# Storing a generated factor with its multiples first and its channels innermost, so that phases are made in place and lag products read a strided moving operand

## The chip, the cores and the metric

The kernel runs on one core of a Trainium2 chip. A core has five engines with queues of their own: TensorE (PE; its weight loads are shown as PEld), VectorE (DVE), ScalarE (ACT), GpSimd (POOL) and SyncE (SP), which issues most of the DMAs. Within a queue the order is fixed; between engines, semaphores order the work. The metric is the device time of one execution in microseconds (us), of which several runs are taken and the median given. Beside them one execution is profiled: every instruction with its engine, source line, tiles, start and duration.

## The reference

Two kinds of layer alternate, twice each: a state-space convolution (S4) and a gated feed-forward net, each behind a layer norm and with a residual. The sequence has L = 2048 steps, the model D = 512 channels, a channel N = 128 states.

```
dt = exp(log_dt)[:, None];  A = A_re + 1j*A_im;  Bc, Cc likewise
P = exp((dt*A)[:, :, None] * arange(L))           # D x N x L
K = einsum("dn,dnl,dn->dl", Cc, P, dt*Bc).real    # the kernel of each channel
y = irfft(rfft(pad(u)) * rfft(pad(K)))[:L] + u*Dskip
x = x + y;   x = x + (silu(n @ w_gate) * (n @ w_up)) @ w_down
```

The change touches only how K is made. It is the same in both convolution layers and is made once.

## The kernel before

A lag l from 0 to 2047 is written as l = 64 b + a', with 32 values of b and 64 of a'. For each state and channel the power exp(dt A l) is the product of a small factor g(b), which also holds C dt B, and a large factor e(a'). K is then a product over the 128 states, which lie on the partitions: for each channel a matmul of g's 32 columns with 64 columns of e, real and imaginary part. These are the **lag products** (`lags`, L486, matmuls at L493 and L494): 64 channels a chunk, two matmuls each, four channels at a time in four column groups of the array; each fp32 matmul stands as two records in the profile. The result is the PSUM tile pk.

The 512 channels are worked in eight chunks of DC = 64. For a chunk `gen_tiles` (L352) takes the tiles re and im (128 states x 64 channels x 65 multiples; two pairs that alternate, tags W0 to W3), mu, xz, mz and tu. Then, in this order:

- `turn_units` (L362), for all channels at the start: th and th32 become the phase of one step and of 32 steps, as integer fractions of a turn. VectorE multiplies by dt (L370), ScalarE copies to integer (L371), VectorE subtracts and scales (L372, L374). Before the change it is called for channels 0 to 127, 128 to 255 and 256 to 511.
- `gen_turns` (L376): VectorE makes five phases in xz (L380) and a ladder of 16 multiples of the large phase in tu (16 multiples x 64 channels): L382, then L386 three times, each doubling the number.
- `gen_trig` (L391): ScalarE makes sine and cosine: for xz (L395 to L401 with 320 elements), then for the sixteen phases into rows 33 to 48 of re and im (L399 absolute value, L400 sine, L401 cosine; 1024 elements), reading tu transposed. `gen_upper` (L404, L407): VectorE adds the sixteenth phase to all of tu. ScalarE does L399 to L401 again, into rows 49 to 64.
- `gen_exp` (L409): ScalarE writes exponentials (the magnitudes) into rows 1 to 32 of re, one row an instruction (L419), and squares (L431). `upper` (L423): squares of them into mu (L425).
- `gen_e` (L434): VectorE multiplies magnitudes and sines into the large factor, rows 0 to 63 of re and im (L440, L443, L445, L448), partly in two halves of the channels.
- `gen_g` (L451): VectorE makes g by doubling (L455 to L483). In chunks 1 to 6 the last product goes to acc (L472), and GpSimd issues a DMA that adds it to the upper half of g (L473).

Behind the lag products ScalarE copies pk to ks (L499), SyncE spreads it through DRAM into kt (L506, L508), and `spectra` (L534) multiplies kt with Fourier constants (L523), two rounds of 32 matmuls a chunk: the first of its own chunk, the second after the next chunk's lag products. Between them lie products for the norm of the weights (L326) and a block of direct products of normalised inputs (L289).

On VectorE, ScalarE, TensorE and SyncE the order is written out by hand. Up to the first lag products it is the sequence of calls from L937 on: statistics of the first 512 rows, units of phase, chunk 0's factors, normalised inputs ne (L281) for the first direct products, chunk 1's phases in between. From then on each step enters a plan with a time (`at`, L994), and the plan is sorted by time; the times only set the order. In chunk c, beginning at t, the lag products of c are issued at t, the factors of c + 1 are finished (`factors`, L1016), and phases and exponentials of c + 2 are made (`prepare`, L1001). So chunk c + 2's phases and exponentials may be written into re and im only when the lag products of c, which read the same buffers, are done.

After the eighth chunk come the weights' splitting, the convolutions of eight blocks and the feed-forward net; this is about three quarters of the time.

Of the kernel before, what the change touches and what calls it, by code (L numbers as in the profile page):

```python
# [14 lines left out]
I32 = mybir.dt.int32  # L15
AF = mybir.ActivationFunctionType
# [6 lines left out]
P = 128  # L23
# [50 lines left out]
def kernel(ctx, tc, x, a_re, a_im, b_re, b_im, c_re, c_im, log_dt, d_skip,  # L74
# [12 lines left out]
    def tl(shape, name, tag, dt=F32):  # L87
        return sb.tile(shape, dt, name=name, tag=tag, bufs=BUFS[tag])
# [263 lines left out]
    def gen_tiles(ch):  # L352
        re = tl([P, DC, 65], "re", f"W{2 * (ch % 2)}")
        im = tl([P, DC, 65], "im", f"W{2 * (ch % 2) + 1}")
        mu = tl([P, DC, 32], "mu", "n")
        xz = tl([P, 3, 5, DC], "xz", "bd")
        mz = mz2[:, ch % 2]
        tu = tl([P, 16, DC], "tu", "z", I32)
        return re, im, mu, xz, mz, tu


    def turn_units(c0, c1):  # L362


        n = c1 - c0
        cs = slice(c0, c1)
        ft = tl([P, 2, 2, n], "ft", "sg")
        fr, fk = ft[:, 0], ft[:, 1].bitcast(I32)
        for i, scale in enumerate((1.0, 32.0)):
            V.scalar_tensor_tensor(fr[:, i], th[:, cs], scale / (2.0 * math.pi), dt[:, cs], OP.mult, OP.mult)  # L370
        A.activation(fk, fr, AF.Copy)  # L371
        V.tensor_tensor(fr, fr, fk, OP.subtract)  # L372
        for i, o in enumerate((th, th32)):
            V.tensor_scalar(o[:, cs].bitcast(I32), fr[:, i], TURN, TURN / 2 - 128.0, OP.mult, OP.min)  # L374

    def gen_turns(ch, ts):  # L376

        re, im, mu, xz, mz, tu = ts
        cs = slice(ch * DC, (ch + 1) * DC)
        V.tensor_tensor(xz[:, 1].bitcast(I32), th[:, cs].bitcast(I32).unsqueeze(1).to_broadcast([P, 5, DC]),  # L380
                        am.unsqueeze(2).to_broadcast([P, 5, DC]), OP.logical_shift_left)
        V.tensor_tensor(tu[:, 0:2], th32[:, cs].bitcast(I32).unsqueeze(1).to_broadcast([P, 2, DC]),  # L382
                        am[:, 0:2].unsqueeze(2).to_broadcast([P, 2, DC]), OP.logical_shift_left)
        yield
        for n in (2, 4, 8):
            V.tensor_tensor(tu[:, n:2 * n], tu[:, 0:n], tu[:, n - 1:n].to_broadcast([P, n, DC]), OP.add)  # L386
            yield
        G.memset(im[:, :, 32], 0.0)
        yield

    def gen_trig(ts):  # L391


        re, im, mu, xz, mz, tu = ts
        A.activation(xz[:, 2], xz[:, 1].bitcast(I32), AF.Sin, scale=-TWO_PI / TURN)  # L395
        tv = tu.rearrange("p m d -> p d m")
        for c, s, turns in ((xz[:, 0], xz[:, 1], xz[:, 1].bitcast(I32)), (re[:, :, 33:49], im[:, :, 33:49], tv),
                            (re[:, :, 49:65], im[:, :, 49:65], tv)):
            A.activation(c, turns, AF.Abs)  # L399
            A.activation(s, turns, AF.Sin, scale=TWO_PI / TURN)  # L400
            A.activation(c, c, AF.Sin, scale=-TWO_PI / TURN, bias=hpi)  # L401
            yield

    def gen_upper(ts):  # L404

        tu = ts[5]
        V.tensor_tensor(tu, tu, tu[:, 15:16].to_broadcast([P, 16, DC]), OP.add)  # L407

    def gen_exp(ch, ts):  # L409


        re, im, mu, xz, mz, tu = ts
# [4 lines left out]
        G.memset(re[:, :, 0], 1.0)  # L417
        for a in sorted(LOW):
            A.activation(re[:, :, a], r_, AF.Exp, scale=32.0 * a)  # L419
            yield  # L420
        yield from squares(ts)

    def upper(ts):  # L423

        A.activation(ts[2][:, :, 1:], ts[0][:, :, 1:32], AF.Square)  # L425

    def squares(ts):

        re = ts[0]
        for st in (2, 4):  # L430
            A.activation(re[:, :, st:33:2 * st], re[:, :, st // 2:17:st], AF.Square)  # L431
            yield

    def gen_e(ts):  # L434


        re, im, mu = ts[:3]
        half = [[t.rearrange("p (g h d) a -> p g h d a", g=4, h=2)[:, :, o] for t in ts[:3]] for o in range(2)]
        for r, m, u in half:
            V.tensor_tensor(m[..., :32], m[..., 64:32:-1], r[..., :32], OP.mult)  # L440
            yield
        for r, m, u in half:
            V.tensor_tensor(r[..., :32], r[..., 64:32:-1], r[..., :32], OP.mult)  # L443
            yield
        V.scalar_tensor_tensor(im[:, :, 33:64], im[:, :, 31:0:-1], -1.0, mu[:, :, 1:], OP.mult, OP.mult)  # L445
        yield
        for r, m, u in half:
            V.tensor_tensor(r[..., 33:64], r[..., 31:0:-1], u[..., 1:], OP.mult)  # L448
            yield

    def gen_g(ch, ts, g):  # L451

        re, im, mu, xz, mz, tu = ts
# [5 lines left out]
        V.tensor_tensor(g[:, :, 0], w_, re[:, :, 64].unsqueeze(1).to_broadcast([P, 2, DC]), OP.mult)  # L459
        V.tensor_tensor(tmp[:, :, 0], w_[:, ::-1], im[:, :, 64].unsqueeze(1).to_broadcast([P, 2, DC]), OP.mult)  # L460
# [25 lines left out]
    def lags(ts, g):  # L486
        re, im = ts[:2]
        pk = pbig([P, 16, 64], "pk")
        for d in range(DC):
            grp, dd = d % 4, d // 4  # L490
            d = 16 * grp + dd
            o = pk[32 * grp:32 * grp + 32, dd, :]
            PE.matmul(o, lhsT=g[:, 0, :, d], rhs=re[:, d, 0:64], start=True, stop=False, tile_position=(0, 32 * grp))  # L493
            PE.matmul(o, lhsT=g[:, 1, :, d], rhs=im[:, d, 0:64], start=False, stop=True, tile_position=(0, 32 * grp))  # L494
        return pk
# [440 lines left out]
    with tc.manual_schedule(engines={mybir.EngineType.Activation, mybir.EngineType.DVE, mybir.EngineType.PE}):  # L936
# [29 lines left out]
        take(fw[1], 1)  # L966
        stats_x = stats(x1, 4, 1.0)
        take(fw[2], 1)
        for g in (gg, ge, gg, ge, gg, ge, gg, ge, gg, tn, gg, tn, gg, tn, gg, tn, gg, tn):
            take(g, 1)  # L970
        tr = gen_trig(ts[1])
        take(tr, 2)
        gen_upper(ts[1])
# [7 lines left out]
        take(tr, 1)  # L981
        take(fw[5], 1)
        for g in (gg, ge, ge, gg, ge, ge):
            take(g, 1)
# [16 lines left out]
        def prepare(c, t):  # L1001
# [7 lines left out]
            for k in range(5):  # L1009
                at(t + 14.4 + 0.4 * k, steps["turns"])  # L1010
            for k in range(3):
                at(t + 17.4 + 2.2 * k, tr)
            at(t + 21.5, lambda: gen_upper(ts[c]))
            at(t + 12.6, steps["exp"], 100)

        def factors(c, t):  # L1016
# [7 lines left out]
            for k in range(4):  # L1024
                at(t + 0.2 + 2 * k, gg, 2)
                if k < 2:
                    at(t + 0.3 + 2 * k, ge, 1)
# [220 lines left out]
```

## Time and profile before

| | us |
|---|---|
| median of 3 runs (lowest, highest) | 1217.76 (1215.12, 1218.78) |
| the profiled execution's own time | 1216.14 |
| its span, first to last instruction | 1214.3 |
| busy: PE / DVE / ACT / POOL | 1097.5 / 1007.3 / 623.5 / 92.8 |
| mean granted TensorE clock | 0.975 |

A row of waits names the engine, tile and line that waited, what released it, then the total in us, the times and the longest. A row of a timeline gives the start, the duration (of several instructions where xN stands at the end), engine, line, operation, output and inputs with shapes, and in brackets how long the engine had been idle and what ended that. A group row gives the count, total busy us and mean ns of one. A stage row gives start:end, length, and each engine's busy us with the number of instructions, then granted clock, DMA share and GB/s. Durations of neighbouring instructions overlap somewhat, so that a pair takes less than the sum of both.

### The profile page before, as it was taken

How to read it: one execution, taken by the hardware profiler on the slowest of the kernel's cores; microseconds unless marked ns; L12 is line 12 of the kernel's file. 1: busy time of each engine (PE TensorE's matmuls, PEld its weight loads, DVE VectorE, ACT ScalarE, POOL GpSimd, SP SyncE). 2: the span in 40 equal slices, each digit the busy share in tenths (PEclk: the TensorE clock that was granted, in tenths of full speed). 3: DMA queues.
4: the chain of work that ended last, by engine and by line, in shares of the span. 5: the costliest groups of instructions: out<-in, count | busy, mean ns of one | idle time of the engine just before them, and what ended most of it. 6: DMA issues, size and time to landing. Idle time of an engine off the chain costs nothing.

```text
span 1214.3 us, 24571 instructions
## 1 busy us (share of the span) xinstructions
PE 1097.5 (90%) x10008; PEld 866.0 (71%) x10008; DVE 1007.3 (83%) x1612; ACT 623.5 (51%) x1205; POOL 92.8 (8%) x151
## 2 busy tenths in 40 slices
PE   0677888889989997999999999989999999999998
PEld 0555676767778684868687777858686776867875
DVE  3878888889879989899899999998997699984221
ACT  6398888993455255355745353564531553325111
POOL 1001111111000001001100000020100010000000
PEclk9988889889989999999999999999999999999999
DMA  5145665665748334732334444433435154312000
GB/s 207 44 149 129 144 142 151 152 174 165 256 140 260 118 117 144 183 116 92 86 113 141 124 157 129 133 102 116 124 120 152 60 133 132 117 57 45 14 23 18
DMA packets 136531, 151.17 MB, mean 124 GB/s; under 512 B 75473, under 2 KB 83665, under 8 KB 136418
## 3 DMA queue, kind: packets, MB, share of 16 engines
q1 hardware_dynamic: 129314, 126.47, 34.8%
q0 software_dynamic: 7104, 23.14, 7.3%
q8 instruction: 78, 1.28, 0.4%
q14 instruction: 35, 0.29, 0.1%
HBM read 101.85 MB, written 31.46 MB: 110 GB/s over the span
## 4 chain that ended last, share of the span: by engine, by line
PE 35%; DVE 27%; issue 4%; DMA 4%; ACT 2%; SPq 1%; POOL 0%; DVEq 0%; ACTq 0%; POOLq 0%
PE pgu L894 6%; PE pgu L895 6%; PE pgu L897 6%; DVE t L762 5%; DVE yk L765 4%; PE py L909 4%; PE py L910 4%; PE py L911 3%; PE pi L781 3%; PE pf L273 3%; DVE yk L762 2%; DMA mix<-nn 2%; DVE z L229 2%; DVE sg L901 2%; DVE bb L229 1%
## 5 line engine op out<-in xcount | busy, mean ns | idle before, releaser
L894 PE MATMUL pgu<-mix,wsl 128*128 128x256 f16 x1280 | 299.7, 273 | 5.3 <-DVE sg L901 2.7
L895 PE MATMUL pgu<-mix,wsl 128*128 128x256 f16 x1280 | 299.7, 273 | 0.0
L897 PE MATMUL pgu<-mix,wsl 128*128 128x256 f16 x1280 | 195.7, 273 | 0.0
L909 PE MATMUL py<-wsl,hh 128*128 128x512 f16 (+1 forms) x352 | 134.3, 381 | 8.8 <-DVE xg L914 7.1
L895 PEld LDWEIGHTS <-wsl 128*128 128x128 f16 x1280 | 125.5, 98 | 22.7 <-issue 6.5
L894 PEld LDWEIGHTS <-wsl 128*128 128x128 f16 x1280 | 125.3, 98 | 16.2
L897 PEld LDWEIGHTS <-wsl 128*128 128x128 f16 x1280 | 125.3, 98 | 15.0
L911 PE MATMUL py<-wsl,hl 128*128 128x512 f16 (+1 forms) x352 | 134.3, 382 | 0.3 <-DVE hl L903 0.3
L910 PE MATMUL py<-wsl,hh 128*128 128x512 f16 x320 | 122.0, 381 | 0.0
L762 DVE TENSOR_TENSOR t<-uu,w 128x1024 f32<-128x1024 f32 x96 | 117.7, 1226 | 2.7 <-DMA w<-wdr 2.5
L765 DVE TENSOR_TENSOR yk<-yk,t 128x1024 f32<-128x1024 f32 x96 | 117.7, 1226 | 0.3
L900 ACT ACTIVATE sg<-pgu,sc 128x512 f32<-128x512 f32 x80 | 54.6, 683 | 119.7 <-PE pgu L897 115.1
L901 DVE SCALAR_TENSOR_TENSOR sg<-pgu,sc,sg 128x512 f32<-128x512 f32 x80 | 60.3, 753 | 55.5 <-ACT sg L900 55.3
L523 PE MATMUL pw<-kt,ek 128*128 128x256 f32 (+1 forms) x384 | 93.6, 381 | 0.0
L902 ACT ACTIVATE hh<-sg 128x512 f16<-128x512 f32 x80 | 50.1, 626 | 77.2 <-DVE sg L901 77.1
L781 PE MATMUL pi<-yl,mix 128*128 128x256 f16 x576 | 78.9, 273 | 5.0 <-DVE yl L229 2.7
L493 PE MATMUL pk<-re,g 128*32 128x64 f32 x1024 | 46.2, 275 | 38.0 <-DVE re L448 33.1
L523 PEld LDWEIGHTS pw<-kt,ek 128*128 128x128 f32 x384 | 70.8, 194 | 8.3
L273 PE MATMUL pf<-z,eh 128*128 128x256 f16 x576 | 74.9, 273 | 0.0
L762 DVE TENSOR_TENSOR yk<-u,w0r 128x1024 f32<-128x1024 f32 x56 | 68.7, 1226 | 1.5 <-ACT u L275 1.5
L493 PEld LDWEIGHTS pk<-re,g 128*32 128x32 f32 x1024 | 41.0, 149 | 39.4 <-issue 39.4
L903 DVE TENSOR_TENSOR hl<-sg,hh 128x512 f16<-128x512 f32 x80 | 55.6, 696 | 15.4 <-ACT hh L902 15.3
(240 smaller groups left out, 2169.2 us busy)
## 6 DMA issues: line engine op xcount, KB each, us to landing
w<-wdr SPq DMA_DIRECT2D x96, 256.0 KB, 2.7
uu<-udr SPq DMA_DIRECT2D x96, 256.0 KB, 3.0
udr<-u POOLq DMA_DIRECT2D x32, 256.0 KB, 2.5
g<-acc POOLq DMA_DIRECT2D x6, 1024.0 KB, 9.0
udr<-u SPq DMA_DIRECT2D x16, 256.0 KB, 2.9
n<-ndr SPq DMA_DIRECT2D x16, 256.0 KB, 4.3
n<-xdr SPq DMA_DIRECT2D x4, 1024.0 KB, 5.7
kdr<-ks SPq DMA_DIRECT2D x6, 512.0 KB, 2.7
```

Of the source, the lines that this page charges most:

```text
L273: PE.matmul(pf[:, o], lhsT=e, rhs=m, start=k == 0, stop=k == len(terms) - 1)
L493: PE.matmul(o, lhsT=g[:, 0, :, d], rhs=re[:, d, 0:64], start=True, stop=False, tile_position=(0, 32 * grp))
L523: PE.matmul(pw[:, i], lhsT=e, rhs=kt[:, :, c + 4 * k0:4 * k1:4, :].rearrange("p g k d -> p k g d"), start=c == 0, stop=c == 3)
L762: V.tensor_tensor(t, uu.unsqueeze(1).to_broadcast([P, 2, 2, HD]), w.unsqueeze(2).to_broadcast([P, 2, 2, HD]), OP.mult)
L765: V.tensor_tensor(yk, yk, t, OP.add)
L781: PE.matmul(pi[:, o], lhsT=e, rhs=m, start=k == 0, stop=k == len(terms) - 1)
L894: PE.matmul(o, lhsT=wgu(wi, k, 0)[:, fs], rhs=nh[:, k], start=k == 0, stop=False)
L895: PE.matmul(o, lhsT=wgu(wi, k, 1)[:, fs], rhs=nh[:, k], start=False, stop=False)
L897: PE.matmul(o, lhsT=wgu(wi, k, 0)[:, fs], rhs=nlo[:, k], start=False, stop=k == 3)
L909: PE.matmul(py[:, r], lhsT=hh[:n, f, rc], rhs=wd(f, 0)[:n], start=f == 0, stop=False)
L910: PE.matmul(py[:, r], lhsT=hh[:n, f, rc], rhs=wd(f, 1)[:n], start=False, stop=False)
L911: PE.matmul(py[:, r], lhsT=hl[:n, f, rc], rhs=wd(f, 0)[:n], start=False, stop=f == FT - 1)
```

## The change

The tiles re, im and mu turn round: multiples first, channels innermost (128 x 65 x 64). The tile tu goes: the ladder stands in rows 33 to 64 of im, as integers, all 32 phases at once (L386 four times), and `gen_upper` goes. ScalarE's L399 to L401 work once on 2048 contiguous elements, the sine in place of its phases. `gen_e` works whole tiles in three of its steps. The lag products read column d of re and im with a step of 64 elements. At the start `turn_units` is called for channels 0 to 63 and 64 to 511 and is cut into steps, whose first (with ScalarE's copy) are issued before chunk 0's sines. In the plan the phases of c + 2 move from t + 14.4 to t + 13.0, in one piece, the sines from t + 17.4 in three steps to t + 17.0 in two, and the exponentials from t + 12.6 to t + 8.3. On the queues of ScalarE and TensorE the order within a chunk stays, apart from the merged steps; on VectorE the ladder's last step stands before L553 instead of L407 behind it, and both halves of L440 become one instruction ahead of g's products.

```diff
 def gen_tiles(ch):
-        re = tl([P, DC, 65], "re", f"W{2 * (ch % 2)}")
-        im = tl([P, DC, 65], "im", f"W{2 * (ch % 2) + 1}")
-        mu = tl([P, DC, 32], "mu", "n")
+        re = tl([P, 65, DC], "re", f"W{2 * (ch % 2)}")
+        im = tl([P, 65, DC], "im", f"W{2 * (ch % 2) + 1}")
+        mu = tl([P, 32, DC], "mu", "n")
-        tu = tl([P, 16, DC], "tu", "z", I32)
...
 def turn_units(ft, c0, c1):
         A.activation(fk, fr, AF.Copy)
+        yield
         V.tensor_tensor(fr, fr, fk, OP.subtract)
...
 def gen_turns(ch, ts):
+        tu = im[:, 33:65].bitcast(I32)
...
-        for n in (2, 4, 8):
+        for n in (2, 4, 8, 16):
             V.tensor_tensor(tu[:, n:2 * n], tu[:, 0:n], tu[:, n - 1:n].to_broadcast([P, n, DC]), OP.add)
...
 def gen_trig(ts):
-        tv = tu.rearrange("p m d -> p d m")
-        for c, s, turns in ((xz[:, 0], xz[:, 1], xz[:, 1].bitcast(I32)), (re[:, :, 33:49], im[:, :, 33:49], tv),
-                            (re[:, :, 49:65], im[:, :, 49:65], tv)):
+        for c, s in ((xz[:, 0], xz[:, 1]), (re[:, 33:65], im[:, 33:65])):
+            turns = s.bitcast(I32)
             A.activation(c, turns, AF.Abs)
             A.activation(s, turns, AF.Sin, scale=TWO_PI / TURN)
             A.activation(c, c, AF.Sin, scale=-TWO_PI / TURN, bias=hpi)
             yield
...
-    def gen_upper(ts):
-        V.tensor_tensor(tu, tu, tu[:, 15:16].to_broadcast([P, 16, DC]), OP.add)
...
 def gen_e(ts):
-        for r, m, u in half:
-            V.tensor_tensor(m[..., :32], m[..., 64:32:-1], r[..., :32], OP.mult)
-            yield
+        V.tensor_tensor(im[:, :32], im[:, 64:32:-1], re[:, :32], OP.mult)
+        yield
...
 def lags(ts, g):
-            PE.matmul(o, lhsT=g[:, 0, :, d], rhs=re[:, d, 0:64], start=True, stop=False, tile_position=(0, 32 * grp))
-            PE.matmul(o, lhsT=g[:, 1, :, d], rhs=im[:, d, 0:64], start=False, stop=True, tile_position=(0, 32 * grp))
+            PE.matmul(o, lhsT=g[:, 0, :, d], rhs=re[:, 0:64, d], start=True, stop=False, tile_position=(0, 32 * grp))
+            PE.matmul(o, lhsT=g[:, 1, :, d], rhs=im[:, 0:64, d], start=False, stop=True, tile_position=(0, 32 * grp))
...
         def turns():
             V.tensor_tensor(rho, rho, dt, OP.mult)
-            turn_units(0, P)
+            take(first, 1)
             take(ex, 14)
-            take(gen_turns(0, ts[0]), 5)
+            take(others, 1)
+            take(first, 1)
+            take(gen_turns(0, ts[0]), 6)
+        ft = tl([P, 2, 2, D], "ft", "ga")
+        first, others = turn_units(ft, 0, DC), turn_units(ft, DC, D)
         stats_x = stats(xe, 4, 1.0, between=turns)
         tr = gen_trig(ts[0])
         take(tr, 2)
-        gen_upper(ts[0])
-        take(tr, 1)
+        take(others, 1)
+        gen_w()
         take(ex, 11)
-        turn_units(P, D // 2)
-        turn_units(D // 2, D)
-        gen_w()
         norm_early(xe, ne, stats_x)
...
 def prepare(c, t):
-            for k in range(5):
-                at(t + 14.4 + 0.4 * k, steps["turns"])
-            for k in range(3):
-                at(t + 17.4 + 2.2 * k, tr)
-            at(t + 21.5, lambda: gen_upper(ts[c]))
-            at(t + 12.6, steps["exp"], 100)
+            at(t + 13.0, steps["turns"], 6)
+            at(t + 17.0, tr, 2)
+            at(t + 8.3, steps["exp"], 100)
```

More of the change, by code (lines that the diff above doesn't have):

```diff
@@ L423, in upper @@
     def upper(ts):
[L425 removed]
+        A.activation(ts[2][:, 1:], ts[0][:, 1:32], AF.Square)
     def squares(ts):
@@ L437, in gen_e @@
         re, im, mu = ts[:3]
[L438 to L448 removed]
+        half = [[t.rearrange("p a (g h d) -> p a g h d", g=4, h=2)[:, :, :, o] for t in (re, mu)] for o in range(2)]
+        V.tensor_tensor(im[:, :32], im[:, 64:32:-1], re[:, :32], OP.mult)
+        yield
+        V.tensor_tensor(re[:, :32], re[:, 64:32:-1], re[:, :32], OP.mult)
+        yield
+        V.scalar_tensor_tensor(im[:, 33:64], im[:, 31:0:-1], -1.0, mu[:, 1:], OP.mult, OP.mult)
+        yield
+        for r, u in half:
+            V.tensor_tensor(r[:, 33:64], r[:, 31:0:-1], u[:, 1:], OP.mult)
             yield
     def gen_g(ch, ts, g):
[L453 removed]
+        re, im, mu, xz, mz = ts
         w_ = w0[:, :, ch * DC:(ch + 1) * DC]
@@ L966 @@
         take(fw[1], 1)
+        take(tn, 6)
         stats_x = stats(x1, 4, 1.0)
         take(fw[2], 1)
-        for g in (gg, ge, gg, ge, gg, ge, gg, ge, gg, tn, gg, tn, gg, tn, gg, tn, gg, tn):
-            take(g, 1)
         tr = gen_trig(ts[1])
         take(tr, 2)
-        gen_upper(ts[1])
+        for g in (gg, ge, gg, gg, ge, gg, gg, gg, gg, gg, gg):
+            take(g, 1)
         for c in range(4):
@@ L980 @@
         take(fw[4], 1)
-        take(tr, 1)
         take(fw[5], 1)
-        for g in (gg, ge, ge, gg, ge, ge):
+        for g in (gg, ge, gg, ge, ge):
             take(g, 1)
```

30 lines of the change are left out of this document (13 added, 17 removed).

## The prediction

> **What bounds the kernel now.** I read the waits first (who waited for whom: us in total, times, longest).
>
> ```profile
> DVE tu L407 <- ACT im L400: 27.2, 8, 4.3
> DVE ft L372 <- ACT ft L371: 9.0, 3, 7.8
> PE pk L493 <- DVE re L448: 33.1, 6, 8.1
> DVE im L440 <- ACT re L431: 3.5, 1, 3.5
> ```
>
> All four lie in the first 300 of 1214.3 us, where the kernels of the eight channel chunks are made. VectorE waits for ScalarE, and TensorE's lag products (pk) wait for VectorE. Next the stages: busy time of PE, PEld, DVE, ACT, POOL, then granted clock, DMA share, GB/s.
>
> ```profile
> 12.00:41.50 29.50, 1.17 (x3) 0.99 (x4) 16.18 (x37) 22.59 (x43) 2.19 (x3) 1.00 0.33 123
> 41.50:75.80 34.30, 29.44 (x128) 25.01 (x126) 30.14 (x46) 20.27 (x23) 1.04 (x1) 1.00 0.21 75
> 110.20:269.80 159.60, 133.86 (x1748) 112.60 (x1748) 140.19 (x174) 140.97 (x279) 23.25 (x43) 0.91 0.61 152
> 269.80:298.70 28.90, 28.87 (x385) 23.54 (x385) 28.42 (x33) 11.92 (x24) 3.20 (x6) 0.93 0.50 156
> ```
>
> The third row holds five chunks: per chunk 31.9 us, DVE 28.0 busy, ACT 28.2, PE 26.8. No engine is full; two that need each other in turn share the limit. The fourth row, the last chunk, has no next-but-one chunk to prepare, and there PE is full. One chunk on VectorE (start, us, idle before in brackets):
>
> ```profile
> 142.79 1.16 DVE L455 TENSOR_TENSOR xz<-xz,mz 128x960 f32<-128x960 f32 x1
> 157.92 2.29 DVE L472 TENSOR_TENSOR acc<-g,xz 128x2048 f32<-128x2048 f32 x1
> 160.12 0.48 DVE L380 TENSOR_TENSOR xz<-th,am 128x320 int32<-128x320 int32 x1
> ...
> 167.21 1.23 DVE L407 CUSTOM_DVE_ANT_0 tu<-tu 128x2048 uint16<-128x2048 uint16 x1 [4.03 <-ACT im L400]
> 168.35 2.36 DVE L443 TENSOR_TENSOR re<-re 128x1024 f32<-128x1024 f32 x2
> 172.76 2.29 DVE L448 TENSOR_TENSOR re<-re,mu 128x992 f32<-128x992 f32 x2
> 174.96 1.16 DVE L455 TENSOR_TENSOR xz<-xz,mz 128x960 f32<-128x960 f32 x1
> ```
>
> L407 adds the upper sixteen phases into the 16-row tile tu, so it must wait until ScalarE has read the lower sixteen (L399, L400). Behind it stand L443 to L448, and TensorE's next lag products stand behind these.
>
> **The change part by part.**
>
> *The reuse of tu goes.* The ladder writes all 32 phases into im rows 33 to 64 before ScalarE starts. L407's 1.23 us come back as a fourth L386 of the same size, so DVE work stays; its wait goes. Eight waits make 27.2 us: 5.4 before the first lag products, 4.3 in the first chunk, 17.5 in the five chunks of the third row (3.5 each). What is late next is VectorE itself.
>
> *ScalarE's reads become contiguous.* Groups by form (total, mean ns):
>
> ```profile
> L399 ACT ACTIVATE re<-tu 128x1024 f32<-128x1024 int32 x16 | 31.4, 1964 | 4.6 <-DVE tu L386 3.2 <-DVE tu L407 1.4
> L401 ACT ACTIVATE re<-re,hpi 128x1024 f32<-128x1024 f32 x16 | 19.0, 1187 | 0.0
> L425 ACT ACTIVATE mu<-re 128x1984 f32<-128x1984 f32 x8 | 15.4, 1919 | 0.0
> L459 DVE TENSOR_TENSOR g<-w,re 128x128 f32<-128x128 f32 x8 | 3.2, 396 | 0.0
> L469 DVE TENSOR_TENSOR g<-g,xz 128x128 f32<-128x128 f32 x8 | 2.3, 292 | 0.2
> ```
>
> L399 reads every element 256 bytes behind the last and takes 1964 ns where L401, contiguous, takes 1187: 0.76 ns more per element. Two rounds of L399, L400 (which reads as L399 does) and L401 cost about 10.2 us a chunk; three operations of 2048 contiguous elements, priced by L425 (1919 for 1984), cost about 5.9. ScalarE falls from 28.2 to below 24 us a chunk, so it no longer ties with VectorE. Its phases now start after the ladder, about 20 us into the chunk, and end at about 26; VectorE asks for that result (L433 of the next chunk) after 29.
>
> *VectorE's own work* shrinks little: L459 and L460 lose their strided read (396 against 292 ns, 0.2 us the pair), two pairs of halves become one instruction each (about 0.07 us each). Together 0.3. DVE floor: 31.9 - 3.5 - 0.3 = 28.1 us a chunk.
>
> *The lag products pay.* Their moving operand re[:, d, 0:64] was contiguous; re[:, 0:64, d] steps 256 bytes. TensorE in the same chunk, and the starts of the other lag products:
>
> ```profile
> 75.79 0.36 PE L493 MATMUL pk<-re,g 128*32 128x64 f32 x7 [3.46 <-DVE g L483]
> 110.17 0.47 PE L493 MATMUL pk<-re,g 128*32 128x64 f32 x8 [8.08 <-DVE re L448]
> 142.03 0.47 PE L493 MATMUL pk<-re,g 128*32 128x64 f32 x8 [5.27 <-DVE re L448]
> 148.56 0.70 PE L523 MATMUL pw<-kt,ef 128*128 128x256 f32 x2
> 167.74 1.46 PE L523 MATMUL pw<-kt,ek 128*128 128x256 f32 x6
> 174.21 0.47 PE L493 MATMUL pk<-re,g 128*32 128x64 f32 x8 [5.00 <-DVE re L448]
> 269.83 0.47 PE L493 MATMUL pk<-re,g 128*32 128x64 f32 x8 [4.94 <-DVE re L448]
> 298.72 0.37 PE L493 MATMUL pk<-re,g 128*32 128x64 f32 x8
> ```
>
> From the end of the lag products (148.5) to the end of the last L523 (169.2) TensorE has 20.6 us of other work and then idles 5.00. With L for the lag products, the chunk lasts the longer of 28.1 and 20.6 + L: the change may make L as much as 7.5 for nothing. The lag products of one chunk, by granted clock (the column before the last two):
>
> ```profile
> 110.00:113.40 3.40, 3.23 (x122) 3.26 (x126) 0.00 (x0) 0.50 0.02 5
> 113.60:115.40 1.80, 1.80 (x129) 1.80 (x123) 0.00 (x0) 1.00 0.04 9
> 298.60:305.00 6.40, 4.58 (x256) 4.30 (x256) 0.14 (x1) 1.00 0.52 142
> ```
>
> The first two rows are one chunk, the third is the last chunk. After the idle stretch the products run at clock 0.50, about 27 ns a record, then at 1.00, 14.0 ns (1.80 us for 129). There are 256 records a chunk: with no penalty and the clock at 1.00, L is 3.6 us, the lower end. A record moves 64 columns; L523's six records of 256 columns last 1.46 us, 0.95 ns a column or 61 ns for 64, so at 14.0 ns the four column groups stream at once, each at 14.0 x 4 / 64 = 0.88 ns a column. No row shows a strided moving operand. The nearest are ScalarE's 0.76 ns per element, and TensorE's own weights, contiguous and at the same 256-byte step (min/median/max ns):
>
> ```profile
> L515 PEld LDWEIGHTS kp<-ks,ident x64: 106/110/111, 284.0 to 308.0; 128*32 128x32 f32 x64
> L493 PEld LDWEIGHTS pk<-re,g x1024: 130/144/178, 75.8 to 304.4; 128*32 128x32 f32 x171
> ```
>
> 34 to 43 ns more for 32 columns is 1.1 to 1.3 ns a column. So a strided column costs 0.88 + 0.76 = 1.64 to 0.88 + 1.2 = 2.08 ns in its stream; times 64, over four streams, 26 to 33 ns a record, L = 6.7 to 8.5. I take 7.5, nearer to ScalarE's row, which moves data and has the clearer difference. The upper end: four streams that don't overlap, 1.64 x 64 x 256 = 27 us. The Vector Engine (DVE) Microarchitecture Reference of the Trainium skill, section 5.2 (Measured stream behaviour on trn2), gives VectorE 1.73 ns per column for one source that hops every element against 1.054; by that ratio L would be about 5.9 (an estimate) and the sum some 3 us lower.
>
> At 7.5 TensorE and VectorE tie at 28.1. In the last chunk TensorE is the bound: 298.72 - 269.83 = 28.9 with lag products of about 5.5 (half the records at either clock) becomes 30.9.
>
> *The start.* VectorE's and TensorE's rows, then a stage (DMA share 0.05: the inputs have been loaded):
>
> ```profile
> 21.93 1.23 DVE L407 CUSTOM_DVE_ANT_0 tu<-tu 128x2048 uint16<-128x2048 uint16 x1 [2.64 <-ACT im L400]
> 31.36 0.42 DVE L372 TENSOR_TENSOR ft<-ft 128x256 f32<-128x256 f32 x1 [7.80 <-ACT ft L371]
> 40.33 1.22 PE L289 MATMUL pf<-xne,ef 128*128 128x256 f32 x2 [29.43 <-DVE xne L281]
> ```
>
> ```profile
> 20.00:24.00 4.00, 0.00 (x0) 0.00 (x0) 1.63 (x3) 3.80 (x4) 0.00 (x0) 1.00 0.05 18
> ```
>
> L371's copies stood in ScalarE's queue behind the phases and exponentials. Now both copies are issued before the phases, and VectorE does the other 448 channels' units right behind the statistics. So 9.0 + 5.4 us of waits go, with some 0.5 of work: L281 and the direct products come about 12 us earlier, the first lag products at 75.8 - 14.9 = 60.9. The direct products (1.2 + 29.4 us of PE in the first two stages) then end near 60 and stay beside it. From the first to the second lag products: 34.4 - 4.3 - 3.5 (L440's wait for exponentials, which come earlier) - 0.3 = 26.3.
>
> *Sum.* 60.9 + 26.3 + 5 x 28.1 + 30.9 = 258.6, against 298.7: 40.1 earlier. The last lag products are themselves longer by 2.9 us (7.5 against 4.6), with the convolution's products queued behind. Everything later is untouched. 1216.1 (the profiled execution, whose span is 1214.3) - 37.2 = 1178.9; the median of the runs is 1217.8, 1.6 more, so about **1180**.
>
> *At nothing:* the ladder now needs im free of the lag products that opened the chunk, which end by 9 us while the ladder starts at 17; if they took over 17, VectorE would wait for them. GpSimd's memsets keep their place behind the same lag products, and nobody waits for them. Rows of re and im that were read in reverse element by element are now reversed by row; L443's pair shows that the reversal costs nothing (2.36 us for 2048).
>
> **The rivals.**
>
> *Strided columns cost more, still overlapped.* If moving columns and strided weights share what reads SBUF at the weights' pace (32 columns in 14.0 ns, 0.44 ns each), a record costs 96 x 0.44 = 42 ns, L = 10.8: chunks of 31.4, the first (one L523 round fewer, some 18 + L) 28.8, the last 34.2, the last lag products +6.2: 60.9 + 28.8 + 157.0 + 34.2 + 6.2 = 287.1 instead of 298.7: 1206 by the median. For it: the weights' rate is only a bound seen, not a limit seen.
>
> *Slower: the streams pass two at a time.* With two streams at 1.64 ns a column, L = 13.4 and TensorE is the bound: 60.9 + 31.4 + 5 x 34.0 + 36.8 + 8.8 = 307.9: about 1227. It decides from L = 12.2, or 48 ns a record. One at a time: over 1330. Against it: at clock 1.00 four strided weight loads and four streams keep 14.0 ns. Advanced Engine Details and Errata of the Trainium skill, section SBUF Cachelines, says that an access that goes to another 16-byte line each time is penalised and that two hits on a line are needed; it gives no size, and 1964 against 1187 ns agrees for ScalarE.
>
> *VectorE's wait is replaced.* The accumulating copy of the upper half of g:
>
> ```profile
> 160.50 1.23 POOL L473 DMA_DIRECT2D g<-acc  x1 [8.44 <-DVE acc L472]
> g<-acc POOLq DMA_DIRECT2D x6, 1024.0 KB, 9.0
> ```
>
> It lands 9.4 to 10.6 us after L472, depending on where the issue is counted from. The work behind L472 that now runs without a stop is 174.96 - 160.12 - 4.03 = 10.8 us up to L455, and L459, one us later, needs the buffer that the copy reads. A copy 3 us slower, with transfers closer together, makes VectorE wait about a us in six chunks: 1186.
>
> **How the numbers follow.** Forecast (L from 3.6 to 9, 1173 to 1191): 0.60, time 1180. Replaced wait, up to 1195: 0.08. Costlier columns, 1191 to 1208: 0.13. Two at a time or worse: 0.17; small mishaps and no change: 0.02. The range 1169 to 1208 leaves out the slower rival and the ends. A measurement of this kernel can tell about 0.3% (3.7 us): faster 0.80, within 0.02, slower 0.18.
>
> **What would show it.** VectorE has no wait on ScalarE between 90 and 260 us; the trig operations of 2048 take about 1.95 us; pk's records run at 26 to 32 ns and one chunk's lag products last 6.6 to 8.3 us; PE's idle before them is under 1 us; chunk starts 28 us apart; the first lag products near 61. Wrong would be: pk over 46 ns a record, lag products after 65 us, or VectorE waiting for the copy or for ScalarE again.

## The result and the profile after

The changed kernel takes **1187.34 us** (median of 4 runs, 1186.22 to 1190.76) against 1217.94 (4 runs, 1215.12 to 1218.78): ratio **0.9757**, 95% interval 0.9731 to 0.9784. That is 30.6 us faster; forecast was 1180, with a range of 1169 to 1208. The profiled execution took 1186.51 us, with a span of 1184.7.

All that was gained lies ahead of the last lag products. Length of each stage in us, from the starts of the lag products (the last column is from the eighth lag products to the span's end):

| kernel | first lags at | first to second | five middle chunks | last chunk | rest |
|---|---|---|---|---|---|
| before | 75.79 | 34.38 | 159.66 | 28.89 | 915.6 |
| forecast | 60.9 | 26.3 | 140.5 | 30.9 | 918.5 |
| after | 60.75 | 28.55 | 145.12 | 31.28 | 919.0 |

The start came out as forecast, the chunks did not quite. First the waits of the changed kernel in its first 270 us (who waited for whom: us in total, times, longest), from which the rows of VectorE for ScalarE have gone:

```profile
DVE cmx L329 <- PE nrm L326: 6.0, 3, 3.3
PE pk L485 <- DVE re L440: 2.8, 1, 2.8
DVE g L451 <- DMA g<-acc: 0.7, 1, 0.7
```

Of TensorE's 33.1 us of waiting before lag products, in six places, one wait of 2.8 us is left. The stages, with busy time of PE, PEld, DVE, ACT and POOL, granted clock, DMA share and GB/s:

```profile
12.00:31.00 19.00, 3.88 (x9) 3.17 (x10) 17.32 (x36) 17.47 (x39) 2.19 (x3) 1.00 0.50 185
31.00:60.75 29.75, 26.95 (x120) 23.21 (x120) 28.04 (x37) 21.07 (x47) 1.04 (x1) 0.99 0.30 106
89.30:234.40 145.10, 145.09 (x1749) 123.09 (x1748) 139.41 (x163) 118.20 (x262) 22.76 (x43) 1.00 0.65 162
234.40:265.70 31.30, 31.30 (x387) 25.72 (x386) 26.44 (x29) 12.30 (x24) 3.27 (x6) 1.00 0.61 187
```

The third row is the five middle chunks: TensorE is busy for 145.09 of 145.10 us, at full clock. Before, no engine was full there (PE 133.86 of 159.60 at clock 0.91); now one is, and it is the one to which the change gave work. ScalarE fell from 28.2 to 23.6 us a chunk. The timeline of the start, and of one chunk on VectorE (start, us, idle before in brackets):

```profile
14.11 0.93 ACT L368 ACTIVATE ft<-ft 128x896 int32<-128x896 f32 x1
26.53 1.91 DVE L281 TENSOR_SCALAR xne<-xne,rs 128x512 f32<-128x512 f32 x4
27.12 1.22 PE L289 MATMUL pf<-xne,ef 128*128 128x256 f32 x2 [16.94 <-DVE xne L281]
...
135.49 0.48 DVE L379 TENSOR_TENSOR xz<-th,am 128x320 int32<-128x320 int32 x1
135.89 0.28 DVE L382 TENSOR_TENSOR im<-tdk,am 128x128 int32<-128x128 int32 x1
136.21 2.74 DVE L386 CUSTOM_DVE_ANT_0 im<-im 128x256 uint16<-128x256 uint16 x4
138.86 0.95 DVE L545 TENSOR_TENSOR spare<-pw,spare 128x768 f32<-128x768 f32 x1
139.73 2.28 DVE L435 TENSOR_TENSOR re<-re 128x2048 f32<-128x2048 f32 x1
```

The direct products start at 27.1 in place of 40.3. The four steps of the ladder stand in one row, and L435 follows without a stop where the kernel before had an idle of 4.03. ScalarE's reads of the phases, grouped by form (total, mean ns):

```profile
L399 ACT ACTIVATE im<-im 128x2048 f32<-128x2048 int32 x8 | 15.3, 1913 | 0.5
L398 ACT ACTIVATE re<-im 128x2048 f32<-128x2048 int32 x8 | 15.2, 1897 | 0.5 <-DVE im L386 0.5
```

2048 contiguous elements take 1.9 us; 1024 strided ones took 1.96. Last, TensorE in the changed kernel: one chunk's lag products, then the rest of the chunk up to the next ones at 148.01 (us, busy, clock, DMA share, GB/s):

```profile
119.15:127.50 8.35, 8.35 (x258) 1.00 0.50 146
127.50:148.00 20.50, 20.50 (x95) 1.00 0.73 174
```

So the lag products of this chunk, L, take 8.35 us, and the chunk is 8.35 + 20.5 = 28.9, all TensorE's.

### The profile page after: what moved, and what is told of

Same layout as the page of the kernel before. It is cut to its first block, busy times and chain, and to the rows that moved or that the text cites. A ratio compares the mean times of both kernels' runs of the same rounds, so it can differ in the third digit from the quotient of the medians.

```text
span 1184.7 us, 24523 instructions
## 1 busy us (share of the span) xinstructions
PE 1117.3 (94%) x10008; PEld 884.8 (75%) x10008; DVE 1006.2 (85%) x1591; ACT 587.1 (50%) x1180; POOL 92.2 (8%) x151
## 4 chain that ended last, share of the span: by engine, by line
PE 37%; DVE 27%; issue 4%; DMA 4%; ACT 2%; SPq 1%; POOL 0%; DVEq 0%; ACTq 0%; POOLq 0%
PE pgu L886 6%; PE pgu L887 6%; PE pgu L889 6%; DVE t L754 5%; DVE yk L757 5%; PE py L901 4%; PE py L902 3%; PE py L903 3%; PE pi L773 3%; PE pf L273 3%; DVE yk L754 2%; DVE z L229 2%; DVE sg L893 2%; DMA mix<-nn 1%; DVE bb L229 1%
## 5 line engine op out<-in xcount | busy, mean ns | idle before, releaser
L902 PEld LDWEIGHTS <-hh 128*128 128x128 f16 (+1 forms) x352 | 34.6, 98 | 46.1 <-issue 10.6
L485 PE MATMUL pk<-re,g 128*32 128x64 f32 x1024 | 65.0, 317 | 2.8 <-DVE re L440 2.8
```

Of the source, the lines that this page charges most:

```text
L902: PE.matmul(py[:, r], lhsT=hh[:n, f, rc], rhs=wd(f, 1)[:n], start=False, stop=False)
```

## The experiments

Three questions: is the lag products' stride what sets the chunks now (1 to 4, 7 to 9); is the bound TensorE's work as such (10, 11); what is the start worth alone (5, 6)? The same stages for every kernel:

| kernel | first lags at | first to second | five middle | last | rest | median |
|---|---|---|---|---|---|---|
| after | 60.75 | 28.55 | 145.12 | 31.28 | 919.0 | 1187.3 |
| 1 moving operand contiguous | 62.36 | 26.34 | 144.20 | 29.42 | 923.4 | 1186.8 |
| 2 moving operand, step 2 | 62.57 | 26.26 | 147.79 | 29.64 | 922.2 | 1190.2 |
| 3 moving operand, step 4 | 62.04 | 27.73 | 145.55 | 31.16 | 923.0 | 1191.2 |
| 4 weights contiguous | 60.98 | 26.22 | 141.26 | 30.24 | 922.1 | 1182.5 |
| 5 start as before | 69.31 | 28.52 | 145.73 | 31.71 | 921.1 | 1198.2 |
| 6 before, new start alone | 65.93 | 34.33 | 158.81 | 28.73 | 917.3 | 1206.7 |
| 7 as 1, filler ahead of the lags | 62.07 | 27.37 | 144.21 | 34.34 | 921.5 | 1189.7 |
| 8 as 1, filler within the lags | 62.55 | 38.63 | 145.57 | 31.65 | 920.3 | 1199.6 |
| 9 both contiguous | 62.30 | 26.30 | 146.57 | 29.18 | 921.1 | 1187.2 |
| 10 after, skip factor in the copy | 60.14 | 27.89 | 141.10 | 29.65 | 906.3 | 1166.6 |
| 11 before, skip factor in the copy | 74.11 | 34.45 | 158.95 | 27.74 | 904.9 | 1202.1 |

In 7 the later starts are those of the filler ahead of the lags. The rest is the same code in after and in 1 to 5 and 7 to 9, and yet it differs by up to 4.4 us from one profiled execution to the next. Totals that lie closer than that are compared by stage. Kernels 2, 3 and 9 were run once each, the others four times.

**1. The moving operand read contiguously.** The lag products read other elements of re and im:

```diff
+        rf, if_ = re.rearrange("p a d -> p (a d)"), im.rearrange("p a d -> p (a d)")
...
-  rhs=re[:, 0:64, d]
+  rhs=rf[:, s0:s0 + 64]          # s0 = 33 * DC + 28 * d; the same for im
```

> The changed kernel, in which every lag product reads its moving operand as 64 neighbouring elements (from the flattened rows 33 to 63 of re and im) in place of one column of 64 rows; weights, order, number of instructions and waits are the same, the elements are other ones, so that K is not the reference's. Theory (the strided moving stream sets the lags' time, and with it the period of the chunks): the 128 records of a chunk's lags fall from 32.5 to 13 to 21 ns (1.7 to 2.7 us in place of 8.3, or what the weight loads leave, up to 3.7), TensorE's need falls under VectorE's 28.1 us, TensorE waits again for the exp factor's last VectorE operation before every lag start, middle chunks 28.0 to 28.3 us, first lags to second 26.3 to 27.5, last chunk 24 to 26, total 1173 to 1180. Rival (VectorE or a transfer sets the chunks and the lags' length is covered): periods stay at 28.7 to 28.9 and the total at 1185 to 1189.

Measured: 1186.83 us (1183.86 to 1190.32), ratio to before 0.9747 (0.9718 to 0.9775), no different from the changed kernel: as a total the theory's number failed. The lags did get shorter, though not to 3.7 us. (The expectation counts 128 records a chunk; the profile shows 256, and at 13 to 21 ns these take 3.3 to 5.4 us.) One chunk's, in this kernel (us, busy, clock, DMA share, GB/s):

```profile
205.86:211.70 5.84, 4.60 (x258) 1.00 0.72 205
```

5.84 us in place of 8.40, of which TensorE is busy for 4.60, and yet the five middle chunks take 144.20. Two of them (30.6 and 30.2 us) gave back what the others (28.5, 27.9, 27.0) had won. Around the fourth lag products, TensorE's timeline and then its windows:

```profile
145.10 0.36 PE L488 MATMUL pk<-re,g 128*32 128x64 f32 x7 [0.57 <-PE pw L518]
151.24 0.22 PE L489 MATMUL pk<-im,g 128*32 128x64 f32 x1 [2.55 <-issue]
```

```profile
145.10:151.40 6.30, 3.75 (x227) 1.00 0.62 172
151.50:158.30 6.80, 6.80 (x50) 0.50 0.51 161
158.40:175.70 17.30, 17.30 (x81) 1.00 0.67 134
175.71:182.20 6.49, 4.57 (x258) 1.00 0.61 182
182.30:189.00 6.70, 6.70 (x16) 0.50 0.59 194
```

TensorE idles for 2.55 us near the end of the lags, for nothing that the profile names ("issue"); right behind that its granted clock is 0.50 for 6.8 us, which costs 3.4. Then TensorE is full again. The next chunk repeats it. Without the spell the chunk would have lasted about 30.6 - 3.4 = 27.2 us (an estimate); the sixth chunk, without a spell, lasts 27.0. So shorter lags opened an idle, and the idle, it seems, took the clock; 7 and 8 put that to the test.

**2 and 3. Steps of 2 and of 4 elements.** As 1, with `rf[:, s0:s0 + 128:2]` and `rf[:, s0:s0 + 256:4]` (s0 = 33 * DC + 24 * d for the latter).

> As the run with neighbouring elements, but the moving operand's 64 elements lie 2 elements (8 bytes) apart; elements other than the reference's, so K is not the reference's. Theory A (the price comes from every element's own place, whatever the distance): records near 32 ns, as with the column of 64 rows (256 bytes apart). Theory B (the price grows with the distance until every element falls into a unit of its own): records between the contiguous run's and 32 ns, near the contiguous run's if a unit holds many elements. Time 1173 to 1180 for B, 1185 to 1189 for A.

> As the run with step 2, with 4 elements (16 bytes) from one to the next; elements other than the reference's. Theory A: records near 32 ns. Theory B: between those of step 2 and 32 ns.

One chunk's lags with step 2, then with step 4:

```profile
209.57:215.50 5.93, 4.89 (x258) 1.00 0.71 202
```

```profile
205.16:213.30 8.14, 8.14 (x258) 1.00 0.52 147
```

8 bytes apart costs next to nothing (5.93 against 5.84; busy 4.89 against 4.60), 16 bytes apart nearly all that 256 bytes do (8.14 against 8.40). That is theory B, with an edge between 8 and 16 bytes: two elements in 16 bytes are read nearly at the pace of neighbours. It agrees with the rule of the Trainium skill (Advanced Engine Details and Errata, section SBUF Cachelines) that at least two hits are needed on each line of 16 bytes; here one hit in place of two costs 2.2 us in 256 records. For the time theory B missed (1190.2 instead of 1173 to 1180): step 2 has the same idles of 2.0 to 2.4 us as 1, and three half-clock spells in the middle chunks.

**4. The weights read contiguously.**

```diff
+        gf = g.rearrange("p i b d -> p i (b d)")
-  lhsT=g[:, 0, :, d]
+  lhsT=gf[:, 0, 32 * d:32 * d + 32]          # the same for i = 1
```

> The changed kernel, in which the lag products' weights are read as 32 neighbouring elements of g in place of one column of 32 rows; the moving operand keeps its column of 64 rows; elements of g other than the reference's, so that K is not the reference's. Theory (the moving stream alone sets the lags, the weight load is beside it): records stay at 32 to 33 ns, a chunk's lags at 8.3 to 8.5 us, periods 28.7 to 28.9, total 1185 to 1189. Rival (moving and weight reads share one budget, so 64 and 32 strided columns add up): records fall by a third to 21 to 23 ns, the lags to 5.5 to 6 us, chunks become VectorE's at 28.1, total 1176 to 1182.

Measured: 1182.52 us, ratio 0.9726 (0.9693 to 0.9758). Stages (PE, PEld, DVE, ACT, POOL, clock, DMA share, GB/s), and one chunk's lags:

```profile
60.98:87.20 26.22, 22.79 (x315) 18.30 (x316) 25.77 (x31) 19.28 (x43) 4.90 (x9) 0.87 0.59 134
87.20:228.46 141.26, 140.98 (x1750) 118.81 (x1749) 139.03 (x164) 117.91 (x266) 23.00 (x43) 1.00 0.69 173
228.46:258.70 30.24, 30.24 (x387) 24.67 (x386) 28.14 (x31) 12.39 (x24) 3.27 (x6) 1.00 0.64 193
...
200.42:208.00 7.58, 7.58 (x257) 1.00 0.56 160
```

Between the two theories: a lag record falls from 32.8 to 29.5 ns, a tenth and not a third. The weights' stride does slow the strided stream, but little. What counts more: with L at 7.5, the value that the prediction took, the chunks are what it forecast. From first to last lags it is 197.72 us here, and 26.3 + 140.5 + 30.9 = 197.7 in the forecast. TensorE is full (140.98 of 141.26) and VectorE nearly (139.03), and the clock stays at 1.00.

**5 and 6. The start alone.** Kernel 5 is the changed kernel with the old `turn_units` calls (three pieces, the later two behind the exponentials); 6 is the kernel before with the new ones:

```diff
-            turn_units(0, P)
+            take(first, 1)
...
-        turn_units(P, D // 2)
-        turn_units(D // 2, D)
+            take(others, 1)          # behind the statistics
```

> The changed kernel with the start of the kernel before: the turns are counted in three pieces in a tile of their own, the other channels' pieces ahead of the weights' generation, as before; tiles, ladder, trig operations and lags are those of the changed kernel. Theory (the start is worth what the sum gave it, the chunks are worth the rest): first lags 9 to 12 us later than the changed kernel's 60.8, at 70 to 73; all later periods unchanged (28.5 first, 28.7 to 28.9 the middle ones, 31.3 the last); total 1195 to 1199. Rival (the start's gain comes from the tiles' new order, not from the pieces): first lags within 2 us of 60.8 and total at 1186 to 1190.

> The kernel before with the changed kernel's start alone: turns counted in two pieces in a shared tile, the other channels' piece after the first trig operations; tiles stay channels first, the ladder of 16 rows and its upper half stay as before. Theory: first lags 8 to 12 us earlier than before's 75.8, at 64 to 68, all periods as before (34.4, then about 32, last 28.9); total 1206 to 1210. Rival (the start gains nothing without the new tiles): 1215 to 1219.

Measured: 5 is at 1198.15 us (1197.34 to 1198.75), ratio to before 0.9852 (0.9835 to 0.987); 6 at 1206.70 (1206.36 to 1207.12), 0.9923 (0.9906 to 0.9941). Waits of VectorE in the first 80 us, in 5 and then in 6:

```profile
DVE ft L371 <- ACT ft L370: 7.5, 3, 6.3
```

```profile
DVE tu L407 <- ACT im L400: 5.8, 2, 3.0
DVE im L440 <- ACT re L431: 3.4, 1, 3.4
```

Each has one of the two groups of waits on ScalarE back, and only that. Kernel 5's first lags come 0.7 us earlier than the expected 70 to 73. The start is worth 8.6 us with the new tiles (69.31 - 60.75) and 9.9 with the old ones (75.79 - 65.93); the other 5 to 6.5 of the 15 us belong to the tiles and the ladder in one piece. Periods stay what the rest of the kernel makes them. Within the tiles' part, the end of the reuse of tu, ScalarE's contiguous reads and the new order in the plan all came together; no kernel here separates them.

**7 and 8. Filling the idle.** If idle takes the clock, work for nothing in its place should keep it. To kernel 1, 8 matmuls ahead of the lags, or 7 between them:

```diff
+        for k in range(8):                                        # 7
+            PE.matmul(pk[:, 0:2, :], lhsT=ident, rhs=ident, start=True, stop=True)
...
+            if grp == 3 and dd % 2 and dd < 15:                   # 8
+                PE.matmul(pk[:, 14:16, :], lhsT=ident, rhs=ident, start=True, stop=True)
```

> The run with the moving operand read as neighbouring elements (K not the reference's), with 8 matmuls of 128 x 128 x 128 fp32 added ahead of every chunk's lags, into a tile that the lags overwrite: about 1.7 us of work for nothing, at the place where TensorE idled. Theory (an idle TensorE is granted half its clock some microseconds later, and this took back what the shorter lags gave): with the idle filled, the clock stays at 1.00 in the middle chunks, periods 28.0 to 28.6 in place of 27.0 to 30.6, and the total is lower by 2 to 7 us than without the filler though work was added. Rival (the half-clock spells have another cause, such as the power of denser streams): spells stay, periods rise to 30 to 32, total 1190 to 1200.

> The run with the moving operand read as neighbouring elements (K not the reference's), with 7 matmuls of 128 x 128 fp32 spread evenly between a chunk's lag products, 1.5 to 1.7 us in all, into columns that later lags overwrite. With the filler ahead of the lags the idle of about 2 us inside them stayed, and the half-clock spells with it. Theory (the idle inside the lags is TensorE's instructions running short, and an idle of 1.8 us or more is what calls a spell): the lags take 6.5 to 7.5 us without an idle over 1 us inside, few or no spells in the five middle chunks, periods 27.5 to 28.6, and first lags to last lags 195 to 200 us. Rival (spells do not hang on idle): spells in two or more of the middle chunks as before, periods there 30 to 32.

Kernel 7 missed: 1189.71 us. The idle ahead of the lags was filled; the one within them stayed in most chunks (1.9 to 2.3 us in three of the five middle ones, "issue"), and so did a spell of half clock there. In one chunk the idle was gone (third lag products):

```profile
119.31:123.55 4.24, 4.24 (x258) 1.00 0.70 196
```

This chunk lasted 26.5 us with the filler, without a spell. Kernel 8's middle chunks, one by one (us, busy, clock, DMA share, GB/s):

```profile
101.18:130.62 29.44, 29.44 (x366) 1.00 0.58 143
130.62:159.69 29.07, 29.07 (x366) 1.00 0.67 165
...
217.67:246.75 29.08, 29.08 (x366) 1.00 0.73 182
```

No idle, and no spell in any of the five: this is the theory's point. The fillers also thin out the stream of the lags, so a rival remains in this run alone, that dense streams call the spells. Kernel 10 below speaks against it: its lags are as slow as the changed kernel's (7.9 to 9.0 us in the middle chunks), and the clock fell there behind idles of 1.78 and 1.99 us. The fillers cost more than estimated (lags of 8.58 us, 2.7 more and not 1.7), so the chunks are TensorE's again, at 29.1. The total of 1199.63 us comes from the first chunk, where TensorE waited 8.2 us for a weight block whose load came late; why it was late was not followed up.

**9. Both contiguous.**

> The changed kernel with moving operand and weights both read as neighbouring elements (other elements of re, im and g, so that K is not the reference's). Theory A (with the moving operand contiguous the lags are bound by the supply of instructions): a chunk's lags stay at 5.7 to 5.9 us, as with contiguous moving operand alone, with the idle inside them. Theory B (the strided weight read then sets them): lags fall to 4 to 5 us. Periods 27 to 31 by how many half-clock spells the idle calls; total 1180 to 1190.

Measured: 1187.21 us, lags of 5.35 to 5.7 us where the idle within them was 1.2 to 1.5 us, and 6.3 or more where it was over 2. Theory A, nearly: contiguous weights bring 0.1 to 0.5 us more, and the idle "issue" stays. The middle chunks show once more what follows:

```profile
117.14:147.17 30.03, 27.92 (x350) 0.89 0.61 150
147.17:177.19 30.02, 27.84 (x351) 0.89 0.62 154
177.19:208.08 30.89, 28.22 (x350) 0.89 0.61 149
208.08:235.17 27.09, 24.72 (x351) 1.00 0.78 201
```

30 us with a spell (clock 0.89 over the chunk), 27 without.

**10 and 11. Other work off TensorE.** In the changed kernel one matmul of a single row adds the skip factor in every second group of spectra. Its place in TensorE's timeline:

```profile
160.48 0.59 PE L515 MATMUL pw<-kt,ef 128*128 128x256 f32 x2
161.00 0.43 PE L517 MATMUL pw<-tdk,one 1*128 1x64 f32 x2
161.37 1.56 PE L515 MATMUL pw<-kt,ek 128*128 128x256 f32 x6
162.76 0.59 PE L515 MATMUL pw<-kt,ef 128*128 128x256 f32 x2
163.20 1.46 PE L515 MATMUL pw<-kt,ek 128*128 128x256 f32 x6
164.49 0.60 PE L326 MATMUL nrm<-sq,onesb 128*128 128x344 bf16 x3
```

With it a group takes 162.76 - 160.48 = 2.28 us, without it 1.73 (164.49 - 162.76): 0.55 each, 4 a chunk. The factor multiplies lag 0 alone, so it can be added there, by GpSimd (kernel 10 on after, 11 on before). The separate maximum of the skip factor in the later scaling goes too, since the lag products then hold it:

```diff
     A.activation(ks, pk.rearrange("p d (c a) -> p a c d", a=4), AF.Copy)
+    G.tensor_tensor(ks[:, 0, 0], ks[:, 0, 0], dm[:, 16 * ch:16 * ch + 16], OP.add)
...
-    if (i, c) == (0, 0) and k0 == 0:
-        PE.matmul(pw[:, 0, 0], lhsT=one[0:1].to_broadcast([1, P]), rhs=dsk[:, ch * DC:(ch + 1) * DC], ...)
```

> The changed kernel with work taken from TensorE that has nothing to do with the lags: the skip factor is added to the kernel's lag 0 by one GpSimd operation of 128 x 16 elements on the copied lag products, in place of 4 matmuls of one row in every chunk's spectra (a group with one takes 2.28 us, one without 1.73, so 2.2 us a chunk). The output is the reference's. Theory (TensorE's need of 28.9 us sets the chunks, with VectorE's 28.1 just behind): middle chunks fall to VectorE's 28.1 and no further while the clock stays at 1.00, last chunk from 31.3 to 29, first to second lags 26 to 27, total 1177 to 1182. With idle on TensorE of about 0.9 us a chunk the clock may fall to half for 3 to 7 us, as it did in the run with neighbouring elements (2.8 us idle a chunk): then some periods are 29 to 30 and the total 1181 to 1187. Rival (VectorE or the copy's way to the spectra sets the chunks): 1186 to 1190, or more if the added operation is late for the spread.

> The kernel before with the skip factor added to the copied lag products by GpSimd in place of 4 matmuls a chunk; the output is the reference's. Theory (before the change VectorE sets the chunks and TensorE has some 5 us of slack, after it TensorE sets them): middle periods stay at 31.5 to 32.2, the last one falls from 28.9 to 27, so the span from first to last lags is 221 to 223 in place of 222.9, where the same edit took 6.3 us off the changed kernel's 204.9. Rival (the edit shortens the chunks whatever sets them): 214 to 218. Behind the last lag products the changed kernel with this edit was 12.7 us shorter, which no theory here foresaw: if that part belongs to the edit alone, it is 900 to 906 us here too (915.6 without), total 1202 to 1207; if it hangs on the order that came with the change, 912 to 918.

Measured: kernel 10 takes **1166.56 us** (1164.58 to 1166.94), ratio to before 0.959 (0.9572 to 0.9608), faster than both, and below its expected 1177 to 1182 by what it gained behind the last lag products; kernel 11 takes 1202.07 (1201.95 to 1204.92), 0.9896 (0.9876 to 0.9915). The five middle chunks of kernel 10 (columns as in 8), and its waits before lag products:

```profile
88.03:229.13 141.10, 131.57 (x1709) 0.99 0.66 169
```

```profile
PE pk L479 <- DMA g<-acc: 5.7, 3, 2.0
PE pk L479 <- DVE re L434: 4.7, 2, 2.9
```

The same of kernel 11:

```profile
108.56:267.51 158.95, 123.15 (x1708) 0.89 0.63 152
```

```profile
PE pk L487 <- DVE re L442: 43.4, 6, 8.3
```

The same edit takes 4.0 us off the middle chunks of the changed kernel, and 0.7 off those of before, where TensorE's waiting grew instead (33.1 to 43.4). Off the last chunk, which TensorE sets in both, it takes 1.6 and 1.2. That answers the question of the bound: TensorE after the change, not before. At 28.2 a chunk kernel 10 meets VectorE's 28.1 and, in three places, the accumulating copy of g; in the middle chunks TensorE waits 5.7 us for the copy and 1.8 for VectorE (the other 2.9 lie ahead of the first lags). Behind the last lag products the edit brings 12.7 us to the changed kernel and 10.7 to the one before, so that part belongs to the edit alone; what in it was not taken apart.

## Why the prediction was right, and where it was off

- **Direction and mechanism: right, shown.** VectorE's waits on ScalarE are gone (27.2 + 9.0 + 3.5 us), the lag products pay, and less than was gained. Kernels 5 and 6 separate the start from the rest; what the single parts of the rest are worth is not shown.
- **The start: right.** First lags at 60.75, forecast 60.9; its parts too, 8.6 to 9.9 us for the units of phase (9.0 of waits, in the forecast) and 5.2 to 6.5 for the tiles (5.4).
- **ScalarE's contiguous reads: right.** 1.90 to 1.99 us a phase operation (forecast about 1.95); ScalarE 23.6 us a chunk (below 24).
- **VectorE's floor of 28.1: right, but not reached in the changed kernel.** Kernels 4 and 10 run at 28.25 and 28.2.
- **The term that was mis-sized: L, the lag products of one chunk, taken at 7.5 us.** It is 8.4 (9.0 in one chunk): 32.8 ns a record, 2.05 ns a strided column in its stream. The bounds were 26 to 33 ns and the choice went to ScalarE's price, since that row "has the clearer difference"; the weight loads' price, the other end (2.08 ns), was the nearer one: it was TensorE's own. That it fits so closely is in part luck: with contiguous weights (kernel 4) the strided column costs 29.5 x 4 / 64 = 1.84 ns, between both rows. As TensorE and VectorE tied at 28.1, every tenth of L beyond 7.5 counted in full: 145.1 - 140.5 = 4.6 us in five chunks, 0.4 in the last, 0.5 in the last lag products. Kernel 4, with L at 7.5, gives the forecast's 197.7 us, and none of these stages is off by more than 0.8 us; so L is what was mis-sized in these chunks.
- **First to second lag products: 28.55 instead of 26.3.** The sum went by VectorE there, and TensorE's need stood in a rival only (18 + L, which is 26.4 with the L that came). TensorE waits in this stage for kt, the lag products spread through DRAM, and does one round of spectra behind it. That wait's end and the stretch from there to the second lag products, in the changed kernel and then in kernel 4:

```profile
79.42 0.67 PE L515 MATMUL pw<-kt,ef 128*128 128x256 f32 x2 [1.06 <-DMA kt<-kdr]
79.42:89.30 9.88, 9.88 (x37) 0.83 0.94 211
```

```profile
78.94 0.67 PE L516 MATMUL pw<-kt,ef 128*128 128x256 f32 x2 [1.16 <-DMA kt<-kdr]
78.95:87.20 8.25, 8.25 (x37) 1.00 0.87 149
```

Of the 2.3 us between the two, 0.7 come from kt (18.67 and 17.96 us after the first lags began) and 1.6 from a spell of 3.4 us at half clock, which in kernel 4 falls earlier. VectorE's sum itself was right: in kernel 9 TensorE waits 0.9 us for VectorE and starts its second lags 26.30 us after the first.

- Together 7.6 us: forecast -37.2 on the profiled execution, measured -29.6 (1216.14 to 1186.51).
- **The forecast's lower end was wrong for another reason.** It held that L down to 3.6 us costs or gains nothing, because VectorE sets 28.1. Kernels 1, 2 and 9 had L of 5.4 to 5.9 where the idle within was short and 6.3 to 7.5 where it was long, and their totals were no lower than with 8.4: TensorE idles within the lags, behind most of the long idles its clock falls, and such a chunk takes 30. The prediction saw the half clock in the kernel before and priced it within the lags; that it also prices slack on TensorE, it didn't see.
- **The rivals.** Columns that share one pace with the weights (42 ns a record): not so; kernel 4 puts the weights' part at 3.3 of 32.8 ns. Streams two at a time (52 ns): not so. VectorE waiting for the copy of g: 0.7 us in the changed kernel; it comes forward in kernel 10, as TensorE's wait (5.7 us).
- **The signs named in advance.** No wait of VectorE on ScalarE between 90 and 260 us: held but for 1.3 us at a copy of spectra. Trig operations of 1.95: held. pk records of 26 to 32 ns and L of 6.6 to 8.3: both just over. PE idle before lags under 1 us: held, after the first. Starts 28 us apart: 28.7 to 29.9. First lags near 61: held.

## What to carry to other kernels

When two engines tie in the sum, the one price that is not in the trace decides the result: carry both of its bounds through to a time (here the row of the same engine came nearer than the cleaner row of another), and write TensorE's need beside VectorE's for every stage. Taking work off a tied engine pays only down to the next bound (2.2 us a chunk gave 0.8), and on TensorE a slack of about 2 us a chunk can cost as much as it saves, through the clock. A cheap place to look is small work on the full engine that another one can do: four matmuls of one row took 2.2 us of each chunk.

## What the runs showed of the hardware

- **A strided moving operand of fp32** takes 22.8 and 23.2 ns a record of 64 columns (idle within the lags included) at steps of 4 and 8 bytes, 31.8 at 16 bytes and 32.8 at 256, with four column groups at once and strided weights. The edge lies between 8 and 16 bytes. Half clock hardly slows the strided stream: the changed kernel's first lags took 8.37 us though 3.1 us of them ran at clock 0.50, where the contiguous records of the kernel before took 27 ns in place of 14.
- **Half-clock spells of TensorE follow idles well under 3 us.** In kernels 1, 2, 7, 9 and 10, from the third lag products on, TensorE idled 19 times for 1.8 to 2.6 us; behind 12 of these idles the clock fell to 0.50 for 3.4 or 6.8 us, from 0.2 to 2 us after the idle. In the chunks from there on with at most 1.75 us of idle (after, 3, 4, 8 and some of the others) it never fell. The Trainium skill (TensorE: Matmul & The Clock Gate, section Why this matters for your kernels) advises against idles over about 3 us; here 1.8 to 2.6 us were enough in 12 cases of 19. A bound can't be read from this: two idles of 1.83 and 2.04 us ahead of the third lag products called no spell, while in the chunk behind the first ones the clock fell 0.4 to 1.9 us after idles of 1.66 to 1.70 us in kernels 4, 8 and 9 (and not after the same idle of the changed kernel).
- **Lag products of 512 instructions** (256 weight loads, 256 matmuls) took no less than 5.35 us in kernels 1, 2 and 9, from the second ones on with an idle of 1 to 2.5 us within, "issue" by the profile. In kernel 7, behind eight long matmuls, they once took 4.24 us without an idle. That TensorE's instructions come no faster otherwise is a guess; no run here shows it.
